# Attention and a spectral mix on one core: bulk loads issued from ScalarE, and the groups of a product kept together

## The chip, the cores and the metric

The kernel runs on one NeuronCore of one Trainium2 chip. The engines are named as in the profile: PE (TensorE: PE for matmuls, PEld for weight loads), DVE (VectorE), ACT (ScalarE), POOL (GpSimd) and SP (SyncE, which here only issues DMAs). The metric is the time of one execution on the device in microseconds, the median of several runs; lower is better.

## The reference

Two independent parts are computed from float32 inputs and put side by side:

```python
def _A_ref(x, wqkv, wo):                     # x: 1 x 2048 x 1024
    H = 32; Dh = D // H; W = 256
    qkv = ((x @ wqkv).reshape(B, S, 3, H, Dh)).transpose(2, 0, 3, 1, 4)
    q, k, v = qkv[0], qkv[1], qkv[2]
    scores = jnp.einsum("bhqd,bhkd->bhqk", q, k) * (Dh ** -0.5)
    mask = (idx[:, None] - idx[None, :] >= 0) & (idx[:, None] - idx[None, :] < W)
    p = _softmax(jnp.where(mask[None, None], scores, -1e9), axis=-1)
    o = jnp.einsum("bhqk,bhkd->bhqd", p, v)
    return o.transpose(0, 2, 1, 3).reshape(B, S, D) @ wo

def _B_ref(x, dft_seq_re, dft_seq_im, dft_hid_re, dft_hid_im):
    a = jnp.einsum("bsd,ed->bse", x, dft_hid_re)
    b = jnp.einsum("bsd,ed->bse", x, dft_hid_im)
    return jnp.einsum("ts,bse->bte", dft_seq_re, a) - jnp.einsum("ts,bse->bte", dft_seq_im, b)
```

Part A is attention with 32 heads of 32 columns, each row looking at the last 256 rows. Part B multiplies a second input by two 1024 x 1024 DFT matrices and then by two 2048 x 2048 ones (cosines and sines).

## The kernel before

**Arithmetic.** Each float32 operand is split into two float16 parts, hi and lo, by a scaled copy on ACT (`hi_op`) and a subtraction on DVE (`lo_op`). A product is then three float16 products (hi hi, hi lo, lo hi). The scales come from searches for the largest value: `top` (DVE, L448) or `mean` (ACT, L989), then a maximum over the partitions by a transpose on PE. Large products are done two by two with seven in place of eight block products; `seven_parts` makes the seven weight operands from two raw tiles (POOL subtracts, ACT L1089 and DVE L1090 split), and `seven` runs the passes over three PSUM accumulators a, b and c, each pass 12 matmuls of 512 columns (or 24 of 256). Between the passes over one accumulator something must read it: a copy from a to c on ACT (L1181), copies or additions on ACT and DVE (L1269, L1272, L1464, L1467). These are the evictions.

**Stages.** First the projections to q, k and v, then part B (units "x": the hidden DFT; units "c": the sequence DFT, one pair of row tiles each, with raw tiles of cosines or sines loaded as they are needed), and last the product with wo. Attention is woven into the second half of the projections and into part B: 256 score blocks, each with scores on PE (L577), masking and maximum on DVE (L588, L593), a bias on POOL (L600), two exponentials on ACT (L603), a hi and a lo part on ACT and DVE (L423, L427), a transposing DMA issued from SP (L612, `t<-hl`), two selects on POOL (L618, L621, tiles z and t), and the product with V on PE (L653). Score tiles have two PSUM buffers.

**Loads.** `load` (L408) issues a DMA from SP. `load_raw` brings a 512 KB raw tile into a ring of six buffers, so a raw load waits until the tile six before it has been read. Its callers are `scan` (the searches over the second input, the DFT weights and wo), `wd_part` (the DFT weights themselves), `u_load` (second input and cosines) and the loads of the projections. Stores of q, k, v and results, the transposes and the loads of q, k and v for attention are issued from SP too; half of the results of part B are added up in DRAM by DMAs issued from POOL (L1561).

**What sets the order.** The kernel doesn't run its operations as they are written. Each is recorded in a `Plan` with an engine, a cost in us, and what it reads and writes. A PE operation is a group of four matmuls of 512 columns. `close` links the operations and gives each a due time, worked back from the order in which the PE work was written. `run` then plays a list schedule: an engine that is free takes, of its operations whose inputs are there, the one that is due first. The order found is emitted, and each engine executes its own list strictly in that order. DMAs get one of eight lanes (`LANES`) in turn, and a DMA waits until the one before it on its lane has landed; before the change `run` modelled this for SP alone. After a PE group `run` adds `DRAIN` (0.17 us) until whatever needs it may start, and before the change that held for the next group of the same product too.

Of the kernel before, what the change touches and what calls it, by code (L numbers as in the profile page):

```python
# [20 lines left out]
P = 128  # L21
# [78 lines left out]
class Plan:  # L100
# [31 lines left out]
    def close(self):  # L132
# [30 lines left out]
        for o in reversed(order):  # L163
            due = o.aim if o.aim is not None else clock + 50.0
            late = self.done(o)
            for x in o.suc:
                due = min(due, x.due - x.cost - late)
            o.due = due

    def run(self):  # L170
# [30 lines left out]
        def start(o, t):  # L201
            nonlocal bus
            e = o.eng
            cost = o.cost
            if o.port:
                other = "POOL" if e == "DVE" else "DVE"
                cost += max(0.0, lock[other] - t)
                lock[e] = t + cost
            free[e] = t + max(cost - TAIL[e], 0.0)
            fin = t + cost  # L210
            if o.dma:
                bus = max(bus, fin) + o.dma[0]
                fin = bus + o.dma[1]
                if e == "SP":
                    lanes.append(fin)
            fin += DRAIN if e == "PE" else SEM
            o.at, o.fin = t, fin
            order.append(o)
            for x in o.suc:
                x.unseen -= 1  # L220
                x.soon = max(x.soon, fin)
                if not x.unseen and x.eng in near:
                    heapq.heappush(near[x.eng], (x.soon, x.n, x))
            put(free[e], "free", o)
            put(fin, "done", o)

        def pick(e, t):
# [4 lines left out]
            while h:  # L232
                item = heapq.heappop(h)
                o = item[2]
                if e == "SP" and o.dma and len(lanes) >= LANES and lanes[-LANES] > t + 1e-9:
                    skipped.append(item)
                    put(lanes[-LANES], "free", o)
                    break
# [26 lines left out]
        while events:  # L265
            t = events[0][0]
            touched = set()
            while events and events[0][0] <= t + 1e-9:
# [4 lines left out]
                elif what == "free":  # L273
                    touched.add(o.eng)
                else:
                    for b in held.get(o, ()):
                        b.todo -= 1
                        if not b.todo:
                            room[b.ring] += 1
                            touched.update(TAIL)  # L280
                    for x in o.suc:
                        x.left -= 1
                        x.avail = max(x.avail, o.fin)
                        if not x.left:
                            if x.avail <= t + 1e-9:
                                heapq.heappush(ready[x.eng], (x.due, x.n, x))
                                touched.add(x.eng)
                            else:
                                put(x.avail, "ready", x)
            for e in touched:  # L290
                pick(e, t)
        assert len(order) == len(self.ops), "not all were placed"
        return order
# [33 lines left out]
def fused_kernel(ctx: ExitStack, tc: tile.TileContext, xa, wqk, wv, wo, xb, wd, cs, out):  # L327
# [76 lines left out]
    def ring_little(n, tag, bufs):  # L404
        return Ring(R, lambda k: small.tile([P, n], F32, tag=tag, bufs=bufs, name=f"{tag}_{k}"), bufs)

    def load(dst, src, kb, w, r=()):
        op("SP", C_ISSUE, lambda: nc.sync.dma_start(dst(), src()), r=r, w=w, dma=wire(kb))  # L408

    def load_raw(src, shape, ring=None):  # L410
        b = (ring or raw_ring).new()
        view = shaped(b, shape)
        load(view, lambda: src, 512, [b])
        return b, view

    def shaped(b, shape):
# [557 lines left out]

    def scan(n):
        key, src, shape, i, k = scans[n]
        b, v = load_raw(src, shape)
        if key == "wo":
            mean(key, b, i)
        else:  # L980
# [37 lines left out]
    sc_ring = ring_little(2, "sc", 6)  # L1018

    def wd_part(p, e, i):  # L1020
        raw = load_raw(wd[p, e, i], [2, CH])
        piece_split(e, i, raw, vwd[:, p, 1, e:e + 1], ("vwd", p, e))

    units = []
# [6 lines left out]
    def u_load(n, j=0):  # L1031
        kind, p, c, i = units[n]
        if kind == "x" and p == 1:
            return
        raws[n, j] = load_raw(xb[8 * c + i] if kind == "x" else cs[p, 2 * i + j, :, 8 * c:8 * c + 8], [ND, P])

    def u_look(n):
        p = units[n][1]
# [604 lines left out]
```

## Time and profile before

| | before |
|---|---|
| median of 3 runs | 1749.88 us (1746.87 to 1755.18) |
| profiled execution, span | 1753.0 us |
| PE busy in the stages 300:700, 700:1100, 1100:1500, 1500:1753 | 390.9 of 400, 386.8 of 400, 387.7 of 400, 244.3 of 253 us |
| ACT busy in the same stages | 272.8, 283.5, 277.6, 102.0 us |
| DMA queues: hardware (SP), software (POOL), share of the 16 DMA engines | 73.2%, 9.0% |

The profile is of one execution of the same program; its page gives the span from the first to the last instruction, and no time of its own beside it. A busy PE in these tables is not a PE at its peak, since the ends of its pipelined matmuls are modelled. The granted clock of PE is 1.00 in all stretches of 50 us but one.

### The profile page before, as it was taken

What the parts mean: (1) busy time and instruction counts of PE and PEld (TensorE: products, weight loads), DVE (VectorE), ACT (ScalarE), POOL (GpSimd) and SP (SyncE); (2) the same over time, 40 slices, a digit from 0 to 9 for tenths busy, and PEclk for the clock granted to TensorE, in tenths of its full rate; (3) what the DMA queues carried; (4) which work ended last, traced back from release to release, by engine and by line L of the source; (5) the groups of instructions that cost most, each with busy time, mean ns of one, the idle gap of its engine ahead of it and who ended that gap; (6) DMA issues with size and microseconds to landing.
All of it is one profiled execution on the core that took longest, in us unless ns stands there. A gap on an engine that the chain in (4) does not pass through costs nothing.

```text
span 1753.0 us, 31898 instructions
## 1 busy us (share of the span) xinstructions
PE 1704.6 (97%) x11671; PEld 912.2 (52%) x11671; DVE 1319.1 (75%) x2213; ACT 1100.7 (63%) x1754; POOL 818.4 (47%) x1021
## 2 busy tenths in 40 slices
PE   9999999999999999999999899999999999999998
PEld 4446687675455444455545455544554554544443
DVE  7988897577987887777897685897775688768641
ACT  6556635566766787776787575677775677654322
POOL 0143401324536664535776565776673677632000
PEclk9999999999999999999999999999999999999999
DMA  6489799989997699898499999759999868885331
GB/s 234 146 323 325 236 316 290 245 228 227 228 288 195 137 213 214 200 287 191 112 173 229 169 225 206 152 110 211 180 210 187 177 118 154 165 215 96 112 105 72
DMA packets 463868, 346.32 MB, mean 198 GB/s; under 512 B 341088, under 2 KB 411744, under 8 KB 463712
## 3 DMA queue, kind: packets, MB, share of 16 engines
q1 hardware_dynamic: 456800, 319.13, 73.2%
q0 software_dynamic: 6912, 25.17, 9.0%
q8 instruction: 91, 1.49, 0.4%
q14 instruction: 65, 0.53, 0.1%
HBM read 173.95 MB, written 96.86 MB: 154 GB/s over the span
## 4 chain that ended last, share of the span: by engine, by line
PE 55%; DVE 11%; POOL 10%; issue 9%; ACT 8%; DMA 6%; SPq 0%; POOLq 0%; DVEq 0%; ACTq 0%
PE m L711 50%; POOL raw L1063 3%; DMA t<-hl 3%; ACT s L603 2%; POOL bias L600 2%; PE pv L653 2%; DVE st L1090 2%; POOL z L618 2%; PE s L577 2%; ACT st L1089 2%; POOL t L621 2%; DVE mx L593 1%; DVE hl L427 1%; ACT hl L423 1%; DMA raw<-in_cs_dram 1%
## 5 line engine op out<-in xcount | busy, mean ns | idle before, releaser
L711 PE MATMUL m<-reg,st 128*128 128x512 f16 x4824 | 1145.7, 379 | 8.7 <-DVE st L1090 3.5
L711 PEld LDWEIGHTS <-st 128*128 128x128 f16 x5448 | 509.8, 97 | 541.4 <-issue 12.3
L603 ACT ACTIVATE s<-s,bias,escs 128x256 f32<-128x256 f32 (+1 forms) x512 | 270.6, 529 | 190.2 <-POOL bias L600 178.9
L600 POOL TENSOR_SCALAR bias<-mx,escs 128x2 f32<-128x2 f32 x256 | 125.8, 492 | 336.7 <-DVE mx L593 285.5
L427 DVE TENSOR_TENSOR hl<-s,hl 128x512 f16<-128x512 f32 (+1 forms) x256 | 171.2, 669 | 115.9 <-ACT hl L423 112.8
L1063 POOL TENSOR_TENSOR raw<-raw,raw 128x512 f32<-128x512 f32 x128 | 182.1, 1423 | 139.1 <-DVE st L1090 128.7
L618 POOL TENSOR_SCALAR_AFFINE_SELECT z<-t 128x512 f16<-128x512 f16 x224 | 172.3, 770 | 71.2 <-DMA t<-hl 54.7
L621 POOL TENSOR_SCALAR_AFFINE_SELECT t<-t 128x512 f16<-128x512 f16 x224 | 171.5, 772 | 10.2
L593 DVE TENSOR_REDUCE mx<-s 128x2 f32<-128x512 f32 (+1 forms) x256 | 170.9, 668 | 5.7
L423 ACT ACTIVATE hl<-s 128x512 f16<-128x512 f32 (+1 forms) x256 | 148.1, 579 | 15.4 <-DMA t<-hl 11.9
L1090 DVE SCALAR_TENSOR_TENSOR st<-raw,sc,st 128x1024 f16<-128x1024 f32 x96 | 135.9, 1419 | 28.8 <-ACT st L1089 28.6
L711 PEld LDWEIGHTS <-reg 128*128 128x128 f16 x1212 | 114.9, 97 | 67.1 <-issue 4.9
L577 PEld LDWEIGHTS <-qk 96*128 96x128 f16 x1056 | 94.8, 98 | 99.8 <-issue 17.7
L588 DVE COPY_PREDICATED s<-upper,old 128x256 f32<-128x256 uint32 x224 | 94.6, 422 | 54.0 <-PE old L577 30.9
L1089 ACT ACTIVATE st<-raw,sc 128x1024 f16<-128x1024 f32 x96 | 109.6, 1144 | 40.6 <-PE m L711 25.0
L711 PE MATMUL m<-reg 128*128 128x512 f16 x480 | 123.0, 379 | 3.5 <-ACT reg L1269 2.4
L653 PE MATMUL pv<-vt,t 128*128 128x65 f16 x1984 | 115.9, 186 | 7.3 <-POOL t L621 7.3
L653 PEld LDWEIGHTS <-t 128*128 128x128 f16 x1984 | 96.4, 97 | 32.3 <-POOL t L621 8.7
L653 PE MATMUL pv<-vt,z 128*128 128x65 f16 (+1 forms) x896 | 100.1, 186 | 7.7 <-POOL z L618 6.9
L577 PE MATMUL s<-qk,qk 96*128 96x128 f16 (+1 forms) x608 | 96.5, 253 | 8.6 <-DVE hl L427 8.1
L711 PE MATMUL m<-xz,st 128*128 128x512 f16 x432 | 100.0, 379 | 0.9 <-DVE st L1090 0.5
L989 ACT ACTIVATE junk<-raw 128x1024 uint8<-128x1024 f32 x88 | 92.7, 1053 | 10.5 <-DMA raw<-in_cs_dram 4.8
(165 smaller groups left out, 2177.4 us busy)
## 6 DMA issues: line engine op xcount, KB each, us to landing
raw<-in_cs_dram SPq DMA_DIRECT2D x64, 512.0 KB, 5.2
qk<-qs SPq DMA_DIRECT2D x192, 128.0 KB, 3.8
out_dram<-ybig POOLq DMA_DIRECT2D x36, 512.0 KB, 6.8
qs<-ybig SPq DMA_DIRECT2D x64, 256.0 KB, 4.4
raw<-in_xb_dram SPq DMA_DIRECT2D x32, 512.0 KB, 5.6
raw<-in_wd_dram SPq DMA_DIRECT2D x32, 512.0 KB, 5.3
raw<-in_wqk_dram SPq DMA_DIRECT2D x22, 512.0 KB, 6.3
vs<-ybig SPq DMA_DIRECT2D x32, 260.0 KB, 4.9
```

Source lines behind the costliest of these rows:

```text
L423: else nc.scalar.activation(dst(), src(), AF.Copy), r=r, w=w)
L427: op("DVE", c_dve(n), lambda: nc.vector.tensor_tensor(dst(), src(), hi(), op=ALU.subtract), r=r, w=w, port=port)
L577: nc.tensor.matmul(dst(j, a, e), qu.t[:, h, i * P:i * P + P], ku.t[:, h, ka:ke], start=True, stop=True, skip_group_check=True)
L593: dve(c_dve(2 * w), lambda: nc.vector.tensor_reduce(mx.t, sv(), axis=AX.X, op=ALU.max, negate=True), r=[(S, 0), (S, 1)], w=[mx])
L600: op("POOL", 0.215, lambda: nc.gpsimd.tensor_scalar(bias.t, mx.t, es, PSHIFT, op0=ALU.mult, op1=ALU.add), r=[mx, ("esc", g // 2)], w=[bias ...
L603: op("ACT", 0.32 + 0.00085 * w, lambda h=h: nc.scalar.activation(sv()[:, h], sv()[:, h], AF.Exp, bias=bias.t[:, h:h + 1], scale=es), r=[bi ...
L618: op("POOL", 0.637, lambda: nc.gpsimd.affine_select(out=z.t, in_=pk(), compare_op=ALU.is_gt, fill=0.0, base=0, pattern=[[0, 4], [-1, P]], ...
L621: op("POOL", 0.637, lambda: nc.gpsimd.affine_select(out=pk(), in_=pk(), compare_op=ALU.is_ge, fill=0.0, base=0, pattern=[[0, 4], [1, P]], ...
L653: nc.tensor.matmul(pvt()[:, r, j, lo:], lhs, vt.t[:, k % QB, at + lo:at + VW], start=a, stop=e, skip_group_check=True)
L711: nc.tensor.matmul(ps.t[:, j * n:j * n + n], lhs(), rhs(), start=first, stop=last, skip_group_check=True)
L1063: lambda: e.tensor_tensor(o(), a(), b(), op=ALU.subtract if sub else ALU.add), r=r, w=w, port=True)
L1090: op("DVE", c_dve(n, True), lambda: nc.vector.scalar_tensor_tensor(dst(1), src(), scl(), dst(0), op0=ALU.mult, op1=ALU.subtract), r=[*r, s ...
```

## The change

Two things are changed. In the planner, a PE operation that depends on another PE operation may start as soon as that one is off the engine, without `DRAIN` (in the due times and in the schedule), and DMAs of ACT take lanes as those of SP do. In the program, `load` and `load_raw` take an engine, and three callers name ACT: `scan`, `wd_part` and `u_load`. These are the loads of the second input (32), of the DFT weights (32), of the cosines and sines (64) and of the searches over wo (8): 136 in all. The loads of the first input, of wqk and wv, of wo itself, and all stores and transposes stay on SP. No matmul, DMA or operation is added or removed. The order is found anew with the new rules.

```diff
@@ close
             late = self.done(o)
             for x in o.suc:
-                due = min(due, x.due - x.cost - late)
+                due = min(due, x.due - x.cost - (0.0 if o.eng == x.eng == "PE" else late))
             o.due = due
@@ run, start
                 fin = bus + o.dma[1]
-                if e == "SP":
+                if e in ("SP", "ACT"):
                     lanes.append(fin)
             fin += DRAIN if e == "PE" else SEM
             o.at, o.fin = t, fin
             order.append(o)
+            if e == "PE":
+                put(t + cost, "next", o)
@@ run, pick
-                if e == "SP" and o.dma and len(lanes) >= LANES and lanes[-LANES] > t + 1e-9:
+                if e in ("SP", "ACT") and o.dma and len(lanes) >= LANES and lanes[-LANES] > t + 1e-9:
@@ run, the loop over events
                 else:
-                    for b in held.get(o, ()):
-                        b.todo -= 1
-                        if not b.todo:
-                            room[b.ring] += 1
-                            touched.update(TAIL)
+                    if what == "done":
+                        for b in held.get(o, ()):
+                            b.todo -= 1
+                            if not b.todo:
+                                room[b.ring] += 1
+                                touched.update(TAIL)
                     for x in o.suc:
+                        if o.eng == "PE" and (x.eng == "PE") != (what == "next"):
+                            continue
                         x.left -= 1
-                        x.avail = max(x.avail, o.fin)
+                        x.avail = max(x.avail, t if what == "next" else o.fin)
...
-            for e in touched:
+            for e in (e for e in TAIL if e in touched):
                 pick(e, t)
@@ loads
-    def load(dst, src, kb, w, r=()):
-        op("SP", C_ISSUE, lambda: nc.sync.dma_start(dst(), src()), r=r, w=w, dma=wire(kb))
-
-    def load_raw(src, shape, ring=None):
+    def load(dst, src, kb, w, r=(), by="SP"):
+        e = nc.scalar if by == "ACT" else nc.sync
+        op(by, C_ISSUE, lambda: e.dma_start(dst(), src()), r=r, w=w, dma=wire(kb))
+
+    def load_raw(src, shape, ring=None, by="SP"):
         b = (ring or raw_ring).new()
         view = shaped(b, shape)
-        load(view, lambda: src, 512, [b])
+        load(view, lambda: src, 512, [b], by=by)
         return b, view
@@ scan
-        b, v = load_raw(src, shape)
+        b, v = load_raw(src, shape, None, "ACT")
@@ wd_part
-        raw = load_raw(wd[p, e, i], [2, CH])
+        raw = load_raw(wd[p, e, i], [2, CH], None, "ACT")
@@ u_load
-        raws[n, j] = load_raw(xb[8 * c + i] if kind == "x" else cs[p, 2 * i + j, :, 8 * c:8 * c + 8], [ND, P])
+        raws[n, j] = load_raw(xb[8 * c + i] if kind == "x" else cs[p, 2 * i + j, :, 8 * c:8 * c + 8], [ND, P], None, "ACT")
```

The first place is PE's list at a "c" unit of part B, around the 80th score tile: the lines that begin with m3, m1 and m0 are matmuls into three product banks (the number before the arrow tells the bank and its user; st tiles are weights of the cosines, reg1 holds the moving operand). Each matmul line stands for a group of four equal ones with their weight loads, of which "..." leaves out the rest. Before:

```order
L711 MATMUL m3_31_7677<-reg1_81,st_59_7452 128x512
...
L577 MATMUL s_80_7885<-qk1_10_6823,qk0_10_7303 128x128
...
L711 MATMUL m3_31_7677<-reg1_81,st_59_7452 128x512
...
L711 MATMUL m1_37_7631<-reg1_81,st_60_7602 128x512
...
L711 MATMUL m3_31_7677<-reg1_81,st_59_7452 128x512
...
L711 MATMUL m1_37_7631<-reg1_81,st_60_7602 128x512
...
L711 MATMUL m0_38_7940<-reg1_81,st_62_7746 128x512
...
L711 MATMUL m1_37_7631<-reg1_81,st_60_7602 128x512
...
L577 MATMUL s_81_7951<-qk1_10_6823,qk0_10_7303 128x256
```

One group of m3 stands ahead of s_80; between s_80 and s_81 the groups of four alternate. After (the lines quoted here are six further down in the file):

```order
L717 MATMUL m3_31_7596<-reg1_81,st_59_7359 128x512
...
L583 MATMUL s_80_7856<-qk1_10_6802,qk0_10_7284 128x128
...
L717 MATMUL m1_37_7562<-reg1_81,st_60_7534 128x512
...
L717 MATMUL m0_38_7898<-reg1_81,st_62_7719 128x512
...
L583 MATMUL s_81_7909<-qk1_10_6802,qk0_10_7284 128x256
```

Now all twelve matmuls of m3 stand ahead of s_80, then come all twelve of m1, and m0 follows with its first four before s_81. The two passes no longer overlap.

The second place is SP's list at the 89th to 91st score blocks (about 708 to 720 us in the trace). The raw tiles are cosines, o and ots are attention's output on its way to DRAM. Before:

```order
L408 DMA raw_121_8513<-in_cs_dram 128x1024
L612 DMA_TRANSPOSE t_89_8536<-hl_89_8511 128x8x128
L1559 DMA out_0_dram<-ybig_83 128x1024
L408 DMA raw_122_8570<-in_cs_dram 128x1024
L612 DMA_TRANSPOSE t_90_8628<-hl_90_8608 128x8x128
L675 DMA_TRANSPOSE o_32_8645<-o_31_8630 128x8x128
L612 DMA_TRANSPOSE t_91_8661<-hl_91_8636 128x8x128
```

After:

```order
L1565 DMA out_0_dram<-ybig_83 128x1024
L618 DMA_TRANSPOSE t_89_8537<-hl_89_8511 128x8x128
L618 DMA_TRANSPOSE t_90_8626<-hl_90_8611 128x8x128
L618 DMA_TRANSPOSE t_91_8646<-hl_91_8632 128x8x128
L681 DMA_TRANSPOSE o_32_8663<-o_31_8634 128x8x128
```

The two loads are gone from SP's list, and the transposes of scores follow each other.

The third place is ACT's list at the same blocks: exponentials (s), hi parts (hl), splits of raw tiles (st, reg1), the copy between accumulators (m3_34). Before:

```order
L423 ACTIVATE hl_89_8511<-s_89_8441 128x512
L1089 ACTIVATE reg1_81<-raw_118_8235,sc_8_8486 128x512
L1089 ACTIVATE st_70_8534<-raw_116_8018,sc_7_8199 128x1024
L1181 ACTIVATE m3_34_8561<-m0_40_8491 128x512
L603 ACTIVATE s_90_8515<-s_90_8515,bias_90_8580,escs_109 128x256 x2
```

After:

```order
L429 ACTIVATE hl_89_8511<-s_89_8438 128x512
L1095 ACTIVATE st_70_8519<-raw_116_7937,sc_7_8193 128x1024
L414 DMA raw_121_8534<-in_cs_dram 128x1024
L1095 ACTIVATE reg1_81<-raw_118_8238,sc_8_8487 128x512
L414 DMA raw_122_8545<-in_cs_dram 128x1024
L1187 ACTIVATE m3_34_8553<-m0_40_8513 128x512
L609 ACTIVATE s_90_8522<-s_90_8522,bias_90_8567,escs_109 128x256 x2
```

The same two loads now stand in ACT's list; raw_122 needs the buffer of raw_116 (six before it), whose last reader is DVE's half of the split st_70, and the copy m3_34 and the exponentials of block 90 are queued behind it.

## The prediction

> **What bounds the kernel now.** I read the head of the page first, then the waits of TensorE, then the places of its longest wait.
>
> ```profile
> span 1753.0 us, 31898 instructions
> PE 1704.6 (97%) x11671; PEld 912.2 (52%) x11671; DVE 1319.1 (75%) x2213; ACT 1100.7 (63%) x1754; POOL 818.4 (47%) x1021
> L711 PE MATMUL m<-reg,st 128*128 128x512 f16 x4824 | 1145.7, 379 | 8.7 <-DVE st L1090 3.5
> 734.57 2.60 PE m L711 x12
> ```
>
> TensorE is busy in 1704.6 of 1753.0 us. Only its 48.4 us without work can go, since the change adds and removes no matmul. The last two rows say how much more than the shown idle time a wait costs: one matmul is shown as 379 ns, but twelve in a row take 2.60 us on the chain, 217 ns each. So the shown end lies 379 - 217 = 162 ns after the point at which the next one could have begun, and each wait is 0.16 us longer than its row says.
>
> The next fence is the waits of TensorE, longest sum first (us in total, times, longest).
>
> ```profile
> PE s L577 <- DVE hl L427: 8.1, 15, 1.5
> PE pv L653 <- POOL t L621: 7.3, 12, 1.4
> PE pv L653 <- POOL z L618: 6.9, 2, 5.2
> PE m L711 <- ACT reg L1269: 4.4, 5, 1.6
> PE m L711 <- DVE st L1090: 3.9, 6, 0.8
> PE old L1046 <- DVE topone L455: 2.2, 3, 1.6
> PE m L711 <- ACT m L1181: 1.4, 3, 0.5
> PE m L1292 <- DVE reg L1287: 1.3, 1, 1.3
> PE m L711 <- DVE reg L1467: 1.2, 2, 0.7
> PE m L711 <- ACT ybig L1464: 1.1, 2, 0.9
> PE m L711 <- DVE ybig L1467: 1.0, 3, 0.5
> PE m L711 <- DVE late L1467: 0.8, 1, 0.8
> PE m L711 <- DVE reg L1272: 0.6, 2, 0.3
> PE m L711 <- ACT reg L1464: 0.6, 1, 0.6
> ```
>
> With 0.16 us for each wait added, they fall into four kinds:
> - **Evictions.** TensorE waits until a PSUM bank has been read (L1269, L1181, L1467, L1464, L1272): 4.4 + 1.4 + 1.2 + 1.1 + 1.0 + 0.8 + 0.6 + 0.6 = 11.1 us in 19 waits, so 14.1 us.
> - **Probabilities.** The products with V wait for the transposed tiles t and z: 14.2 us in 14 waits, 16.4 us.
> - **Scores.** A new score tile waits until the softmax two tiles back has left its PSUM: 8.1 us in 15 waits, 10.5 us.
> - **Weights** (L1090): 3.9 us in 6 waits, 4.9 us.
>
> No kind is over 1% of the time. The longest wait is here:
>
> ```profile
> 959.35 3.18 SPq L408 DMA_DIRECT2D qk<-qs  x3
> 962.62 6.72 SPq L612 DMA_TRANSPOSE t<-hl  x1
> 979.14 0.63 POOL L618 TENSOR_SCALAR_AFFINE_SELECT z<-t 128x512 f16<-128x512 f16 x1 [6.46 <-DMA t<-hl]
> 979.83 0.24 PE L653 MATMUL pv<-vt,z 128*128 128x65 f16 x1 [5.23 <-POOL z L618]
> 950.00:1000.00 50.00, 43.89 (x301) 22.49 (x299) 32.32 (x65) 30.96 (x52) 29.40 (x36) 0.93 1.10 183
> ```
>
> One transposing DMA held SP's sequencer for 6.72 us, its tile came late, and TensorE stood for 5.23 us. The last row (busy time of the engines, then the granted clock, 0.93 in these 50 us) adds 50 x 0.07 = 3.5 us of lost clock. So the probabilities cost 16.4 + 3.5 = 19.9 us.
>
> **The change part by part: the order on TensorE.** The planner used to hold a group of four matmuls back by its drain time after the group before it in the same product; it put another product's group there. Now a product's three groups of a pass follow each other, as the first place of the order shows. In the whole program the matmuls on the four product banks stood in 1722 pieces and now stand in 878. No matmul is added. What changes is when a bank is done: two products that alternate end within one group (four matmuls, 0.87 us) of each other and want two evictions at once; products in a row end a pass of 2.60 us apart. An eviction costs this:
>
> ```profile
> L1464 ACT ACTIVATE ybig<-m,fu x96: 662/679/704, 608.8 to 1609.9; 128x512 f32<-128x512 f32 x96
> L1181 ACT ACTIVATE m<-m x61: 559/582/597, 84.4 to 1730.8; 128x512 f32<-128x512 f32 x61
> ```
>
> Two of them (1.3 us) don't fit into 0.87 us; one fits into 2.60 us with 1.9 us to spare. I take 70% of the 14.1 us away: **-10 us**. The bounds are 0 (other work on ACT and DVE was ahead of the eviction, and still is) and -14.1. When a wait for a bank goes, the scores are late next; they get no room from this.
>
> **The loads.** 136 loads leave SP's queue for ACT's.
>
> ```profile
> L408 SPq DMA_DIRECT2D raw<-in_cs_dram x64: 327/370/1635, 463.9 to 1565.2; - x64
> L408 SPq DMA_DIRECT2D raw<-in_xb_dram x32: 328/334/890, 210.7 to 783.4; - x32
> L408 SPq DMA_DIRECT2D raw<-in_wd_dram x32: 327/351/911, 246.7 to 1011.4; - x32
> L612 SPq DMA_TRANSPOSE t<-hl x256: 1188/1242/7972, 271.4 to 1519.7; - x128
> SPq L612 <- DVE hl L427: 169.5, 100, 7.1
> SPq L408 <- DVE st L1090: 100.6, 43, 26.5
> SPq L408 <- DVE top L448: 32.9, 28, 4.7
> ```
>
> By the medians (ns, in the middle of each triple) they hold SP for 64 x 0.370 + 32 x 0.334 + 32 x 0.351 = 45.6 us, and the eight of wo, taken like cs, for 3.0: 48.6 us. The last two rows are SP's waits ahead of loads, until a raw buffer has been read. A transpose queued behind such a load waits with it. But the row above them says that SP mostly waits for the transposes' own input (169.5 us), so the queue is seldom what makes them late. I take 40% off the 19.9 us, chiefly the long wait and its clock: **-8 us**. The bounds: 0, if the transposes are slow in the DMA engines, and -19.9.
>
> On the ACT side no row shows a DMA's issue, so SP's durations stand in. 48.6 us of issue over 256 score tiles is 0.19 us for each tile's chain. ACT is idle for 1753.0 - 1100.7 = 652 us, much of it ahead of the exponentials:
>
> ```profile
> ACT s L603 <- POOL bias L600: 178.9, 136, 4.7
> ```
>
> That idle time is the cover. It is gone where the chain is late already: 15 late scores x 0.19 = **+3 us**. The bounds are 0 (issued while ACT waits) and +48.6 (all of it on the path, which 652 idle us make remote).
>
> **The added wait.** ACT takes its instructions in order, and its load now waits for the last reader of its buffer. The second and third place of the order show one such load with the copy m3_34 behind it. This is what the trace has there:
>
> ```profile
> 709.01 1.15 ACT L1089 ACTIVATE st<-raw,sc 128x1024 f16<-128x1024 f32 x1
> 710.63 0.58 ACT L1181 ACTIVATE m<-m 128x512 f32<-128x512 f32 x1 [0.47 <-PE m L711]
> 710.48 1.69 DVE L1090 SCALAR_TENSOR_TENSOR st<-raw,sc,st 128x1024 f16<-128x1024 f32 x1
> 712.21 0.33 SPq L408 DMA_DIRECT2D raw<-in_cs_dram  x1
> ```
>
> ACT was free at 710.16, the buffer's last reader on DVE ended at 712.17, and SP issued the load at 712.21. With the load in ACT's row, the copy would begin at about 712.54 instead of 710.63, 1.9 us late; the score chain's exponentials and the evictions behind it wait too. The slack that a pass leaves an eviction, 1.9 us, just covers this. The longest of the 28 waits for DVE's searches (4.7 us) would not be covered: 4.7 - 1.9 = 2.8 us. Taking one such wait: **+3 us**. The bounds are 0 and, if each of the 71 waits of the two rows moved to ACT and went on to TensorE, +133.5 us; I stay near 0, because these rows are of an SP that often has nothing else to do and hold other loads too, while ACT comes to its loads later.
>
> The eight semaphore lanes of the DMAs are shared by both engines now; a DMA waits until the one eight places before it in the order has landed. The page's list of DMA issues has the landing last:
>
> ```profile
> raw<-in_cs_dram SPq DMA_DIRECT2D x64, 512.0 KB, 5.2
> t<-hl SPq DMA_TRANSPOSE x256, 4.3
> ```
>
> At 5.2 us eight lanes take a DMA every 0.65 us, and SP needs 0.3 to 1.2 us to issue one, so they seldom bind; I cost it at 0, within the added wait's upper bound.
>
> **Sum:** -10 - 8 + 3 + 3 = -12 us. The span goes from 1753.0 to 1741.0. The profiled span is 3.1 us over the median of the timed runs, 1749.88; so the time is 1749.9 - 12 = **1738 us**.
>
> [...]
>
> **The rivals.**
> [...]
> 2. *The next wait takes over.* Evictions come in time, but TensorE then stands for the scores, whose chain through DVE, POOL and ACT got no shorter. Half of the -10 and half of the -8 come back: -9 + 6 = -3, **1747 us**. 13%.
> 3. *ACT's row is blocked* (slower). Where a load waits longer than the 1.9 us of an eviction's slack, evictions and exponentials wait behind it. If 14 of the 71 waits (one in five) each exceed it by 2 us, +28 takes the place of the last +3: -18 + 3 + 28 = +13, **1763 us**. It decides from about twelve such waits (-15 + 24 = +9). For it: DVE is the busiest engine beside TensorE (75%) and is what the loads wait for. Against: ACT's 652 us of idle time. [...] 17%.
> 4. *SP was the brake.* All of evictions and probabilities go: -14 - 20 + 6 = -28, **1722 us**. 15%.
>
> **How the numbers follow.** My forecast has 40%. A measurement can tell about 0.5% (8.7 us) from no change. Faster by more: the forecast and rival 4, 55%. Within it: rivals 1 and 2, 28%. Slower: rival 3, 17%. The range reaches from a little under rival 4 to rival 3, with its upper tail cut: **1716 to 1764 us**.
>
> **What would show it.** In the changed kernel's waits of TensorE, the eviction rows should sum to about 4 us in place of 11, the t and z rows to under 9 in place of 14, the row for the scores to 8 to 11, and no window should have a clock under 0.99 in mid-kernel. ACT should show waits ahead of its loads of 30 to 60 us in sum, few over 2 us. SP's transposes should follow the end of their input more closely. The forecast is wrong if the scores' row grows by over 8 us (rival 2 or 3), or if a transpose still takes 6 us to issue (rival 1).

## The result and the profile after

The changed kernel takes 1766.1 us (median; its runs lie between 1762.4 and 1772.3) against 1748.4 us for the kernel before beside it: a ratio of **1.010, 95% interval 1.007 to 1.013**. It is slower by 1%, where 1738 us was forecast. Three disturbed runs, one of the changed kernel (1809 us) and one each of two experiments below (old order from ACT, 1804 us; large part from ACT, 2194 us), are left out of all medians and ratios. The profiled execution of the changed kernel took 1762.4 us, its span is 1760.7 us.

The first lines of the page of the changed kernel (span; busy time of the engines), then its DMA queues (packets, MB, share of 16 engines):

```profile
span 1760.7 us, 31889 instructions
PE 1705.0 (97%) x11671; PEld 911.3 (52%) x11671; DVE 1309.9 (74%) x2213; ACT 1097.6 (62%) x1754; POOL 804.7 (46%) x1021
q1 hardware_dynamic: 437216, 247.82, 61.9%
q10 hardware_dynamic: 19584, 71.31, 13.3%
```

TensorE is busy for as long as before (1704.6), so the loss is time in which it stands. The second hardware queue, q10, is new: the 136 loads, 71 MB, travel on it. It is called ScalarE's row of queues from here on, and q1 SP's. What TensorE waits for, in the changed kernel (us in total, times, longest):

```profile
PE s L583 <- DVE hl L433: 17.4, 13, 8.1
PE m L717 <- DVE st L1096: 6.2, 9, 1.4
PE m L717 <- ACT m L1187: 5.5, 5, 2.0
PE pv L659 <- DVE o L670: 3.5, 6, 1.5
PE pv L659 <- POOL t L627: 3.5, 7, 1.1
PE m L717 <- DVE ybig L1473: 2.6, 4, 1.8
PE pv L659 <- POOL z L624: 2.1, 2, 1.5
```

The probabilities (t and z) fell from 14.2 to 5.6 us, but the scores (first row) rose from 8.1 to 17.4. Two waits make 12.4 us of it. The longest, 8.1 us, ends at 1215 us. The rows of POOL, ACT and TensorE there (in brackets the idle time before, and what ended it):

```profile
1210.71 0.63 POOL L624 TENSOR_SCALAR_AFFINE_SELECT z<-t 128x512 f16<-128x512 f16 x1 [9.32 <-DMA t<-hl]
1212.14 0.62 POOL L606 TENSOR_SCALAR bias<-mx,escs 128x2 f32<-128x2 f32 x2
1212.44 1.11 ACT L609 ACTIVATE s<-s,bias,escs 128x256 f32<-128x256 f32 x2 [8.50 <-POOL bias L606]
1215.42 0.58 PE L583 MATMUL s<-qk,qk 96*128 96x256 f16 x2 [8.09 <-DVE hl L433]
```

POOL's select z stands 9.32 us for a late transpose, and the biases of later score tiles stand behind it in POOL's list, though DVE had finished both of their maxima by 1204.7 us. The exponentials wait for the biases, and the scores for the softmax. The second longest wait, 4.3 us, ends at 954 us. First SP's list around it (a row with a count spans several instructions), then ACT's:

```profile
933.66 6.99 SPq L618 DMA_TRANSPOSE t<-hl  x2
940.75 0.53 SPq L414 DMA_DIRECT2D vt<-vs  x1
941.37 16.80 SPq L618 DMA_TRANSPOSE t<-hl  x3
```

```profile
938.58 0.33 ACTq L414 DMA_DIRECT2D raw<-in_cs_dram  x1
939.01 0.47 ACTq L414 DMA_DIRECT2D raw<-in_cs_dram  x1
940.46 0.33 ACTq L414 DMA_DIRECT2D raw<-in_wd_dram  x1
...
952.41 0.60 ACT L429 ACTIVATE hl<-s 128x512 f16<-128x512 f32 x1 [4.84 <-DMA t<-hl]
```

ACT issues its three loads in under half a microsecond each. But the hi part at 952.41 us stands 4.84 us, until an earlier transpose has read its buffer hl (issued at 937.79 us, landed at 952.33). Without that hi part the softmax doesn't finish, the score PSUM isn't free, and TensorE stands:

```profile
953.79 0.58 PE L583 MATMUL s<-qk,qk 96*128 96x256 f16 x2 [4.31 <-DVE hl L433]
```

So at both places the chain that ends in the row of the scores begins at a transpose that lands late. The experiments ask whose doing that is.

### The profile page after: what moved, and what is told of

It reads as the page before. It is cut to its first block, busy times and chain, and to the rows that moved or that the text cites. A ratio compares the mean times of both kernels' runs of the same rounds, so it can differ in the third digit from the quotient of the medians.

```text
span 1760.7 us, 31889 instructions
## 1 busy us (share of the span) xinstructions
PE 1705.0 (97%) x11671; PEld 911.3 (52%) x11671; DVE 1309.9 (74%) x2213; ACT 1097.6 (62%) x1754; POOL 804.7 (46%) x1021
## 4 chain that ended last, share of the span: by engine, by line
PE 51%; DVE 14%; DMA 10%; POOL 9%; issue 8%; ACT 7%; SPq 0%; ACTq 0%; POOLq 0%; DVEq 0%
PE m L717 46%; DMA t<-hl 5%; POOL raw L1069 3%; DVE st L1096 2%; PE pv L659 2%; POOL bias L606 2%; ACT s L609 2%; POOL z L624 2%; DVE hl L433 2%; PE s L583 2%; ACT st L1095 1%; DVE mx L599 1%; POOL t L627 1%; DVE reg L436 1%; ACT hl L429 1%
## 5 line engine op out<-in xcount | busy, mean ns | idle before, releaser
L717 PE MATMUL m<-reg,st 128*128 128x512 f16 x4824 | 1112.0, 379 | 13.8 <-DVE st L1096 6.0
L717 PEld LDWEIGHTS <-st 128*128 128x128 f16 x5448 | 517.1, 98 | 583.5 <-issue 14.0
L606 POOL TENSOR_SCALAR bias<-mx,escs 128x2 f32<-128x2 f32 x256 | 122.2, 477 | 357.1 <-DVE mx L599 281.4
L624 POOL TENSOR_SCALAR_AFFINE_SELECT z<-t 128x512 f16<-128x512 f16 x224 | 170.8, 765 | 86.2 <-DMA t<-hl 72.3
L717 PE MATMUL m<-reg 128*128 128x512 f16 x480 | 118.0, 385 | 0.0
L583 PE MATMUL s<-qk,qk 96*128 96x128 f16 (+1 forms) x608 | 96.8, 253 | 17.8 <-DVE hl L433 17.4
L659 PE MATMUL pv<-vt,t 128*128 128x65 f16 x1984 | 98.8, 185 | 3.6 <-POOL t L627 3.5
L659 PEld LDWEIGHTS <-t 128*128 128x128 f16 x1984 | 88.2, 96 | 18.1 <-issue 5.4
L659 PE MATMUL pv<-vt,z 128*128 128x65 f16 (+1 forms) x896 | 87.9, 185 | 5.6 <-DVE o L670 3.5
```

The source lines that it names most:

```text
L583: nc.tensor.matmul(dst(j, a, e), qu.t[:, h, i * P:i * P + P], ku.t[:, h, ka:ke], start=True, stop=True, skip_group_check=True)
L606: op("POOL", 0.215, lambda: nc.gpsimd.tensor_scalar(bias.t, mx.t, es, PSHIFT, op0=ALU.mult, op1=ALU.add), r=[mx, ("esc", g // 2)], w=[bias ...
L624: op("POOL", 0.637, lambda: nc.gpsimd.affine_select(out=z.t, in_=pk(), compare_op=ALU.is_gt, fill=0.0, base=0, pattern=[[0, 4], [-1, P]], ...
L659: nc.tensor.matmul(pvt()[:, r, j, lo:], lhs, vt.t[:, k % QB, at + lo:at + VW], start=a, stop=e, skip_group_check=True)
L717: nc.tensor.matmul(ps.t[:, j * n:j * n + n], lhs(), rhs(), start=first, stop=last, skip_group_check=True)
```

## The experiments

All ratios are to runs of the kernel before, taken beside them on the same chip, with 95% intervals. "Plan" is the order that the planner finds; "issue" is which engine's instruction starts a load. KB is what ScalarE issues of each load of 512 KB.

| run | plan | loads issued from | ratio |
|---|---|---|---|
| planner alone | new rule, loads on SP | SP | 0.9998 (0.9976 to 1.0020) |
| loads alone | old rule, loads on ACT | ACT | 1.0348 (1.0321 to 1.0375) |
| old rule, loads from SP | old rule, loads on ACT | SP | 1.0042 (1.0008 to 1.0075) |
| **new order, loads from SP** | the changed kernel's | SP | **0.9938 (0.9919 to 0.9957)** |
| old order, loads from ACT | of before | ACT | 1.0242 (1.0202 to 1.0282) |
| cosines from ACT | the changed kernel's | ACT 64, SP 72 | 1.0107 (1.0041 to 1.0172) |
| all but cosines from ACT | the changed kernel's | ACT 72, SP 64 | 1.0038 (1.0005 to 1.0071) |
| sliver from SP (control) | the changed kernel's | SP twice | 0.9967 (0.9953 to 0.9980) |
| sliver from ACT, 4 KB | the changed kernel's | ACT and SP | 1.0011 (0.9995 to 1.0026) |
| small part from ACT, 64 KB | the changed kernel's | ACT and SP | 1.0001 (0.9985 to 1.0017) |
| half from ACT, 256 KB | the changed kernel's | ACT and SP | 1.0018 (0.9994 to 1.0042) |
| 384 KB from ACT | the changed kernel's | ACT and SP | 1.0059 (1.0035 to 1.0084) |
| large part from ACT, 448 KB | the changed kernel's | ACT and SP | 1.0124 (1.0092 to 1.0155) |
| two DMAs, rows of 2048 B, SP | the changed kernel's | SP twice | 0.9909 (0.9883 to 0.9934) |
| two DMAs, rows of 2048 B, ACT | the changed kernel's | ACT twice | 1.0174 (1.0148 to 1.0200) |
| two DMAs, rows of 512 B, SP | the changed kernel's | SP twice | 1.0003 (0.9981 to 1.0026) |
| two DMAs, rows of 512 B, ACT | the changed kernel's | ACT twice | 1.0303 (1.0279 to 1.0326) |

**The two halves of the change.** The planner's edits with all loads left to SP, and the loads moved with the old rule on groups kept:

```diff
     def load(dst, src, kb, w, r=(), by="SP"):
+        by = "SP"
         e = nc.scalar if by == "ACT" else nc.sync
```

> All of the planner's edits, but all loads issued from SP as before. Three theories of the 1.0% loss. Ring theory (bulk loads on a second queue make the transposes land later): the loads are back on one queue, so this is 5 to 15 us faster than before, and the median from issue to landing of a transpose is 4.4 us as before. ACT theory (ACT's list is held up by its loads): also 5 to 15 us faster than before. Order theory (groups of one product in a row leave the scores less room): 10 to 20 us slower than before, as the changed kernel is, with the wait of the scores for hl near 17 us.

It measured 1747.75 us, no difference (0.9998); none of the three theories had that.

```diff
-                due = min(due, x.due - x.cost - (0.0 if o.eng == x.eng == "PE" else late))
+                due = min(due, x.due - x.cost - late)
...
-            if e == "PE":
-                put(t + cost, "next", o)
...
-                        if o.eng == "PE" and (x.eng == "PE") != (what == "next"):
-                            continue
```

> The 136 loads issued and planned on ACT, but the planner holds a group back by its drain time as before, so that products alternate. Ring theory and ACT theory: slower than before by 15 to 30 us (the changed kernel's loss plus the gain of the order). Order theory: within 8 us of before.

It measured 1812.55 us: worse than the whole change, and than any theory had it. So the two parts don't add up, and the loads are the part that costs.

**Order and issue apart.** A recorded load has an engine for the plan and an engine that issues it. These two runs set them apart: the changed kernel's plan with the loads issued from SP, and the plan of before with the same loads issued from ScalarE. The first edit is to the changed kernel, the second to the kernel before, where the same three callers name ACT.

```diff
     def load(dst, src, kb, w, r=(), by="SP"):
-        e = nc.scalar if by == "ACT" else nc.sync
+        e = nc.sync
```

> The changed kernel's plan to the last operation (loads planned as ACT's), but at emission each of the 136 loads goes onto SP's queue. Ring theory: faster than the changed kernel by 10 to 20 us, and the transposes' median landing back at 4.4 us. ACT theory: faster by 10 to 20 us too, but the transposes' landing stays as in the changed kernel, 4.7 us or more. Order theory: within 8 us of the changed kernel.

```diff
-    def load(dst, src, kb, w, r=()):
-        op("SP", C_ISSUE, lambda: nc.sync.dma_start(dst(), src()), r=r, w=w, dma=wire(kb))
...
+    def load(dst, src, kb, w, r=(), by="SP"):
+        e = nc.scalar if by == "ACT" else nc.sync
+        op("SP", C_ISSUE, lambda: e.dma_start(dst(), src()), r=r, w=w, dma=wire(kb))
```

> The plan of before to the last operation (loads planned as SP's), but at emission each of the 136 loads goes onto ACT's queue. Ring theory: slower than before by 10 to 20 us, with transposes landing 0.3 us or more later in the median and no long waits on ACT. ACT theory: slower by 20 us or more, since nothing in this plan allows for ACT's issue, with ACT's idle time ahead of loads and exponentials up. Order theory: within 8 us of before.

The first measured **1739.56 us**, 27 us under the changed kernel and more than any theory gave it; the second 1787.88, 38 us over the kernel before, which only the ACT theory had allowed. The new order by itself gains 0.62%; issuing the loads from ScalarE loses 1.6% in the new order (1.010 against 0.9938) and 2.4% in the old. The first run beats both kernels, and its waits of TensorE show what is gone:

```profile
PE s L583 <- DVE hl L433: 6.8, 9, 4.3
PE m L717 <- ACT m L1187: 5.4, 5, 2.0
PE m L717 <- DVE st L1096: 3.8, 5, 1.4
PE pv L659 <- POOL t L627: 3.0, 6, 1.1
```

The same stretch of its SP list, with the same work in the same order (the loads again between the second and the third transpose), and the hi part that had waited 4.84 us:

```profile
925.49 5.37 SPq L618 DMA_TRANSPOSE t<-hl  x2
930.95 0.53 SPq L414 DMA_DIRECT2D vt<-vs  x1
931.57 1.54 SPq L414 DMA_DIRECT2D raw<-in_cs_dram  x2
933.20 0.68 SPq L414 DMA_DIRECT2D raw<-in_wd_dram  x1
933.98 8.89 SPq L618 DMA_TRANSPOSE t<-hl  x3
```

```profile
939.44 0.60 ACT L429 ACTIVATE hl<-s 128x512 f16<-128x512 f32 x1
```

Three transposes are issued in 8.89 us in place of 16.80, and the hi part waits for nothing. The transpose that it needs lands 6.6 us after its issue here and 14.5 us after it in the changed kernel, though in both the three loads are issued behind it. In the changed kernel the first of these loads, issued 0.8 us after the transpose, landed 2.0 us before it; here none did. That one load overtook the transpose is not shown to be the reason why it was late, since the loads were late too: 12 to 16 us from issue to landing, against 7.5 to 8.5 here (see the last section).

What TensorE and POOL feel of the transposes, as the group of z selects on POOL (busy, mean ns | idle before, by what), in the changed kernel and in the run with the loads from SP:

```profile
L624 POOL TENSOR_SCALAR_AFFINE_SELECT z<-t 128x512 f16<-128x512 f16 x224 | 170.8, 765 | 86.2 <-DMA t<-hl 72.3 <-DMA qk<-qs 3.9 <-PE pv L659 3.3
```

```profile
L624 POOL TENSOR_SCALAR_AFFINE_SELECT z<-t 128x512 f16<-128x512 f16 x224 | 173.3, 777 | 49.1 <-DMA t<-hl 37.6 <-PE pv L659 5.2
```

POOL waits 72.3 us for transposes with the loads on ScalarE's row, 37.6 with them on SP's (and 54.7 in the kernel before). From the issue and landing times of the 256 transposes in the trace: the mean is 5.48 us against 4.86, and 39 against 11 take longer than 8 us. It is the tail that grew, not the middle (median 4.7 and 4.6), so the sign that was to tell the theories apart, the median, doesn't. The same holds for the old order: the median is 4.3 us with the loads from either engine, and 36 transposes against 17 take longer than 8 us.

**Where the planner's gain comes from.** One more pairing, the plan with the loads on ScalarE by the old rule, issued from SP (edits of the second and third run together):

> The loads planned on ScalarE, but with the old rule that keeps the groups of one product apart, and all loads issued from SyncE. With the new rule the same was 0.62% faster than the kernel before. If the new rule (groups follow each other) is what gains: no faster than the kernel before, 1748 us or more. If the plan that no longer charges SyncE for the loads is what gains: 1737 to 1743 us, as with the new rule. If both are needed or share it: 1744 to 1748.

It measured 1760.45 us (ten runs between 1746.8 and 1769.5), 0.4% slower than before. So neither the rule on groups alone (0.9998) nor the plan that doesn't charge SP (1.0042) gains; together they give 0.9938. Beside the run with the loads alone, which has the same plan, it also gives a third price for issuing from ScalarE: 3.1% (1.0348 against 1.0042).

**ScalarE held, or the row of queues.** Issuing from ScalarE does two things: ACT stops for the buffer (51 us in sum ahead of its 136 loads in the changed kernel) and for the issue (0.33 us each), and the bytes, 71 MB, travel on another row of queues (q10). Cutting each load into two DMAs, one for each engine, keeps the first the same and varies the second:

```diff
-        load(view, lambda: src, 512, [b], by=by)
...
+            def two():
+                nc.scalar.dma_start(b.t[:, :128], flat[:, :128])
+                nc.sync.dma_start(b.t[:, 128:], flat[:, 128:])
+            op("ACT", C_ISSUE, two, w=[b], dma=wire(512))
```

> The changed kernel's plan; each of the 136 loads is cut in two: ACT issues the first 128 of 1024 columns (64 KB, with the same wait for the buffer and the same place in its list), SP the other 896 (448 KB). ACT theory (the issue and the wait in ACT's list cost the time): as slow as the changed kernel, 1755 to 1775 us, whoever carries the bytes. Ring theory (the bytes on a second queue beside the transposes cost it): near the new order from SP, 1735 to 1750 us, a few us of it for 136 more DMAs, with the 95th percentile of the transposes' landing back under 9 us.

The other has the engines exchanged:

> The same cut with the sides exchanged: SP issues the first 128 columns, ACT the other 896, so as many DMAs as in the run beside it, as many on ACT, and only the bytes differ. Ring theory: slower than the run beside it by 15 to 30 us, about the changed kernel. ACT theory: within 8 us of the run beside it.

They measured 1751.06 and 1771.69 us: the first between the ranges of the two theories (its transposes land in 7.8 us at the 95th percentile, as the ring theory asked), the second where the ring theory had it. The DMAs, ACT's issues (medians of 335 to 352 ns) and the places of its waits are the same; **20.6 us** come from which row carries the bulk. POOL's selects in the two (small part first):

```profile
L633 POOL TENSOR_SCALAR_AFFINE_SELECT z<-t 128x512 f16<-128x512 f16 x224 | 172.3, 772 | 52.3 <-DMA t<-hl 41.8
```

```profile
L633 POOL TENSOR_SCALAR_AFFINE_SELECT z<-t 128x512 f16<-128x512 f16 x224 | 172.3, 772 | 74.9 <-DMA t<-hl 57.7
```

With the bulk on ScalarE's row POOL waits 57.7 us for transposes in place of 41.8, 20 of them in place of 12 take longer than 8 us to land, and TensorE's wait for the scores grows from 9.3 to 17.2 us. So here, too, at least part of the cost comes by late transposes. Then the sliver (columns 8 and 1016 in place of 128 and 896), its control with both DMAs from SP, half and half, and 384 with 128 KB:

> The changed kernel's plan; each of the 136 bulk loads is cut, and ScalarE issues the first 8 columns (4 KB), SyncE the other 1016. ScalarE waits for the buffer and issues a DMA as in the changed kernel, but almost no bytes travel on its row of queues. Two-cost theory (ScalarE's issue and wait cost about 10 us by themselves, the bytes on its row come on top): 1748 to 1752 us, 9 to 13 more than the same two DMAs from SyncE. Row theory (only what travels on the second row costs): within 4 us of the same two DMAs from SyncE.

> Control: the same two DMAs of 8 and 1016 columns, both from SyncE. By all theories 1739 to 1744 us, as with two halves from SyncE (1739).

> Each bulk load cut into halves, one issued from ScalarE and one from SyncE, in the changed kernel's plan. With 64 KB of each load on ScalarE's row the time was 1751 us, with 448 KB 1773. Two-cost theory, the cost of the row in proportion to its bytes: 1751 + 22 x 192 / 384 = 1762 us, 1757 to 1767 allowed. If any large transfer on the second row costs the whole: 1770 or more. If only transfers near the whole load cost: under 1756.

> Each bulk load cut, 384 KB of it issued from ScalarE and 128 KB from SyncE, in the changed kernel's plan. Over the kernel before, 4, 64 and 256 KB from ScalarE gave +0.1, 0.0 and +0.2%, 448 KB +1.2%. If the cost of the row rises steadily from 256 KB on: +0.7 to 1.0% (1763 to 1769 us). If it appears only when nearly the whole load is on ScalarE's row: under +0.4% (1758 us). If it appears as soon as more than half of the load is there: +1.1% or more (1770 us).

The medians are 1754.45, 1745.29, 1755.94 and 1763.28 us. Holding ACT, wait and issue together, costs 1754.45 - 1745.29 = **9.2 us** (0.44%) with almost no bytes on its row. The difference is what the two-cost theory had (9 to 13 us), though both runs are a little slower than their forecasts. Whole loads cost 1.62% from ScalarE (1.010 against 0.9938); without the 0.44, 1.18% or some 20 us are left for the row, and the pair with 64 and 448 KB gives 1.23% (1.0124 - 1.0001).

How the row's cost grows with the bytes isn't settled. Counted from the sliver, nothing outside the noise is added at 64 and 256 KB, 0.5% at 384 and 1.1% at 448 KB, as if the cost came with the last half. But the sliver is a high base: its control from SP is 0.3% slower than whole loads from SP (0.9967 against 0.9938). The control that fits the half, two halves from SP, is the run with rows of 2048 B in the table, 0.9909. Against it the half costs 1.1%, and against whole loads 0.8%. Without 0.44 for holding ACT, 0.4 to 0.65% are left for half of the bytes, which a steady rise would give too. The cuts at 64 and 384 KB have no control of their own. The half came out 1 us under the 1757 to 1767 expected of a steady line, and 384 KB at 0.59% under the 0.7 to 1.0% of one; neither miss refutes it.

**Which loads.** Whole loads again, but only the 64 of cosines, or only the other 72, from ScalarE (`load` takes ScalarE for these alone):

> The changed kernel's plan, with only the 64 loads of cosines and sines emitted from ACT, the other 72 from SP. They are the ones that run beside the transposes all through part B. Ring theory: most of the loss is here, 10 us or more over the new order from SP (1745 us or more). ACT theory: about half of the loss (64 of 136 issues), some 12 us.

> The changed kernel's plan, with the 72 other loads (second input, DFT weights, searches) emitted from ACT and the cosines from SP. Ring theory: little loss over the new order from SP, under 10 us, since half of these loads lie in the stage before the transposes begin or in its first part. ACT theory: about half of the loss or more, 12 us and up, since the searches' waits are the ones in a row.

They measured 1768.04 and 1754.13 us. The cosines alone cost as much as all. But the other 72 cost some 15 us over the new order from SP (1.0%), where the ring theory had under 10 and the ACT theory 12 or more. The two parts together cost more than the whole, so they can't be read as shares of it. The cosines carry 33.6 MB over the row, about as much as the halves in the run with half of each load (35.7 MB), which cost less (1.0018 against 1.0107, with intervals that just touch): so the sum of bytes alone hardly sets the cost. Whether it matters that the loads are whole, or that all of these bytes travel beside the transposes, isn't shown.

**Length of rows.** Two DMAs for each load, with rows of 2048 B (two halves) or of 512 B (every other 128 columns), each from ScalarE and from SP. One more theory, that the length of the rows sets the cost of the transfers from ScalarE, had under 10 us for short ones:

```diff
+                nc.scalar.dma_start(d3[:, 0::2], s3[:, 0::2])
+                nc.scalar.dma_start(d3[:, 1::2], s3[:, 1::2])
```

> The changed kernel's plan, with each of the 136 bulk loads cut into two DMAs of 256 KB that take every other 128 columns, so that a row of a packet is 512 B in place of 4096 B; both issued from ScalarE. Read against the run with the same two DMAs issued from SyncE. [...] Bytes theory (what counts is that 71 MB come over a second row of queues at all): 1.2 to 2% slower than from SyncE (21 to 35 us), as with long rows. Issue theory (ScalarE is held by its DMA issues, 0.33 us each, 136 more of them): 45 us or more slower than from SyncE with either length of row.

> The changed kernel's plan, with each of the 136 bulk loads cut into two DMAs of 256 KB with rows of 2048 B, both issued from ScalarE. [...] Issue theory: 45 us or more slower than from SyncE.

> Control: the short rows of 512 B, both DMAs issued from SyncE in the changed kernel's plan. If short packets and 136 more DMAs cost nothing, 1740 us as with whole loads from SyncE; I expect 1745 to 1765, since the same bytes come in eight times as many packets. Transposes are behind whole loads in one row of queues here, by all theories.

> Control: the rows of 2048 B, both DMAs issued from SyncE in the changed kernel's plan. Tells what 136 more DMAs cost by themselves. If the 11 us between the run with the small part from ScalarE (1751 us) and the one with whole loads from SyncE (1740 us) come from the number of DMAs, this one is at 1751 too; if they come from ScalarE's issue and wait or from the 64 KB on its row, this one is at 1740.

From SP they measured 1752.78 and 1739.23 us, from ScalarE 1808.68 and 1786.37: ScalarE costs 56 us with short rows and 47 with long. Shorter rows don't help, so the theory that had under 10 us for them falls. The issue theory met its number, but not by itself: it says nothing of the 20.6 us above. The issues do add up, though. Those of the cosines in the two runs from ScalarE, long rows first, each with the second DMA of a load below the first (ns: min/median/max):

```profile
L423 ACTq DMA_DIRECT2D raw<-in_cs_dram x64: 334/334/603, 487.0 to 1589.7; - x64
L424 ACTq DMA_DIRECT2D raw<-in_cs_dram x64: 334/453/1505, 487.3 to 1590.8; - x64
```

```profile
L425 ACTq DMA_DIRECT2D raw<-in_cs_dram x64: 374/375/2408, 498.6 to 1608.4; - x64
L426 ACTq DMA_DIRECT2D raw<-in_cs_dram x64: 374/557/4381, 499.1 to 1609.8; - x64
```

A load holds ACT for 0.79 us here, 0.93 with short rows (1.2 for the DFT weights and the second input), and 0.33 in the changed kernel. If 0.33 us is worth 9.2 us, 0.79 is worth about 22: of the 47 us some 25 remain, near the 20 above. That is an estimate, and it leaves out that ACT also stands longer ahead of its DMAs here: by the start times in the traces 74 us in sum with long rows and 59 with short ones, against 51 in the changed kernel, once 8.5 us until a transpose had landed. No run separates these for the two kernels.

## Why the prediction was wrong

**The step that failed is the second: "The loads", -8 us.** It took the leaving of 136 loads from SP's queue as a relief for the transposes, with bounds of 0 and -19.9. The sign was wrong: with ScalarE's wait and issue held the same, the bulk on the other row costs some 20 us, at least in part through transposes that land later. I had set the lower bound at "slow in the DMA engines: 0" and had no bound on the other side, although nothing in the trace of before showed a second hardware row at work (q1 alone, 73.2%); that was the unknown price, and it was bounded from one side only.

The row that the step leaned on was also misread. The step counted on the leaving of the loads to relieve the transpose that held SP for 6.72 us. In the kernel before, these steps of 2 us around it (engines, granted clock, DMA share, GB/s last) show another thing:

```profile
966.00:968.00 2.00, 2.00 (x11) 0.88 (x9) 2.00 (x4) 1.41 (x4) 1.79 (x2) 1.00 1.11 245
968.00:970.00 2.00, 2.00 (x12) 0.88 (x9) 0.81 (x3) 1.45 (x4) 2.00 (x3) 1.00 2.88 76
970.00:972.00 2.00, 2.00 (x13) 1.09 (x12) 1.63 (x3) 1.93 (x3) 2.00 (x3) 1.00 0.07 16
972.00:974.00 2.00, 2.00 (x11) 0.88 (x9) 0.38 (x2) 0.94 (x3) 0.68 (x1) 1.00 1.48 99
```

For 6 us the DMA engines moved 16 to 99 GB/s where they had moved 245. What held that transpose back, 16.4 us from the start of its issue to its landing at 979.0 us, lay at least in part in these 6 us. That fewer loads on SP's list would have ended them isn't shown, and the changed kernel has such a stretch too (last section).

**The order on TensorE (-10 us).** The forecast wanted the evictions (ACT's and DVE's readers of the product banks) down from 11.1 to about 4 us. They are at 9.5 in the changed kernel (the same five kinds of lines) and at 6.7 with the planner's edits alone, which gained nothing in time. The rule was worth nothing with the loads planned on SP, and 1.0% with them planned on ScalarE and issued from SP (1.0042 against 0.9938). The new order as a whole measured 1739.6 us with the loads from SP, near the forecast of 1738, but by another sum: mostly the probabilities, 14.2 to 3.0 us, not the evictions (8.5). So that agreement is luck and bears out neither term.

**The ACT side (+3 and +3).** Holding ACT was put at +6 in two terms and measured 9.2 us: the mechanism is right, the size a little small. The waits ahead of ACT's loads came as forecast (30 to 60 us in sum, few over 2): by the start times in the trace of the changed kernel, ACT stands 51 us in sum ahead of its 136 loads, four times over 2 us and 2.8 at most. The list of ACT's waits shows none of this, because it leaves out instructions that only issue DMAs. One place (the second row spans two loads):

```profile
965.44 1.15 ACT L428 ACTIVATE reg<-raw,vwd 128x1024 f16<-128x1024 f32 x1
968.33 2.46 ACTq L414 DMA_DIRECT2D raw<-in_cs_dram  x2
971.38 0.69 ACT L1470 ACTIVATE reg<-m,fu 128x512 f32<-128x512 f32 x1 [4.79 <-PE m L717]
```

ACT was free at 966.59 us and its loads began at 968.33 and 970.46; the whole gap of 4.79 us is put down to TensorE. The issue is 0.33 us for each load, as assumed from SP. How the 9.2 us divide between wait and issue isn't shown; they were measured with the sliver, where ACT stands 66 us ahead of its DMAs, so for whole loads they may be a little high.

**The rivals.** Rival 3 (ACT's row blocked, slower) gave 1763 us, close to the profiled 1762.4, by a mechanism that the trace doesn't bear out: of ACT's waits ahead of its loads five exceed the slack of 1.9 us, by 0.9 at most (two loads in a row stand up to 3.5 us together), where fourteen were to exceed it by 2; and with ACT as much occupied the time falls to 1751 us when the bulk stays on SP's row. Rival 2 named the place, the scores' row growing by more than 8 us (it grew by 9.3), but not the sign of the time, nor the reason, since at the two longest waits the chain stood for transposes. Rival 1, which put the -8 at 0, was nearer on the loads, since no relief came; its sign fired too: a transpose took over 6 us to issue (11.4 us from 941.37 us on). Rival 4 asked for all evictions and probabilities to go; even in the fastest order 8.5 + 3.0 us of them remain. The clock was forecast at 0.99 or more in all windows; it is lower where the two longest waits lie:

```profile
950.00:1000.00 50.00, 44.11 (x303) 21.93 (x303) 35.20 (x67) 31.39 (x51) 28.52 (x39) 0.97 1.12 211
1200.00:1250.00 50.00, 41.53 (x314) 21.64 (x312) 32.21 (x73) 31.58 (x54) 31.79 (x41) 0.90 1.13 186
```

## What to carry to other kernels

Moving bulk loads to another engine's DMA queue was here not only a question of the time that an issue takes (0.33 us). Small transposes that a chain waits for were under way beside the loads; the other row cost some 20 us of 1750, more than the 9.2 us of holding ACT, and no relief showed. When a change plans work on one engine and issues it there, the two can be set apart in an experiment; here the plan alone was 0.6% faster and the issue 1.6% slower. And a resource that the trace of before never shows at work needs a bound on both sides of nothing. Last, a list of waits shows only what it counts: the time that ACT stood ahead of its loads had to be read from the start times.

## What the runs showed of the hardware

**Stalls of the DMA engines.** The stretch of the changed kernel in which the late transposes were under way, in steps of 2 us (GB/s last):

```profile
940.00:942.00 2.00, 2.00 (x11) 0.94 (x10) 1.93 (x8) 0.00 (x0) 0.92 (x2) 1.00 0.93 193
942.00:944.00 2.00, 2.00 (x14) 1.02 (x13) 2.00 (x5) 1.84 (x4) 0.56 (x2) 1.00 2.05 64
944.00:946.00 2.00, 2.00 (x12) 0.98 (x11) 1.39 (x4) 2.00 (x4) 1.68 (x3) 1.00 1.05 37
946.00:948.00 2.00, 2.00 (x24) 1.12 (x23) 1.49 (x2) 1.54 (x3) 0.00 (x0) 1.00 0.39 30
948.00:950.00 2.00, 1.48 (x22) 0.84 (x19) 0.00 (x0) 0.00 (x0) 0.00 (x0) 1.00 1.00 293
```

Three bulk loads, a small one, two transposes and a store were under way, and for 6 us only 30 to 64 GB/s moved. The same set of transfers, in the run with the loads from SP and over the 13 us that it takes there, moves at 238 GB/s:

```profile
929.60:942.60 13.00, 12.97 (x109) 6.96 (x106) 11.85 (x25) 8.91 (x17) 8.71 (x12) 1.00 1.03 238
```

The packets of 4096 B on ScalarE's row that began between 942 and 948 us took 2.1 us each in the mean, against a median of 0.16 us over the whole run. So at this place throughput was lost, and it wasn't only the order of transfers that changed. The kernel before shows such a stall (16 to 99 GB/s for 6 us) with all its loads on SP's row, too, so one came without a second row. What starts one is open, and so is how much of the row's 20 us comes from such stalls.

**Small parts.** The 136 more DMAs on SP show no cost where both are 256 KB (1739.2 us against 1739.6 with whole loads), and cost some 5 us where one is a sliver with rows of 32 B (1745.3; the intervals of the ratios, 0.9953 to 0.9980 and 0.9919 to 0.9957, just overlap).
